# Linear attention, then a mixture of experts: attention outputs as dimensions by tokens in 64-by-32 tiles of TensorE, denominators apart by way of DRAM, and another order of the last stage

## The chip, the cores and the metric

The kernel runs on one core of a Trainium2 chip. The metric is the device time of one execution in microseconds; lower is better. All tensors are float32.

## The reference, cut to what matters

2048 tokens of 512 dimensions go through a pre-normed attention with 32 heads of 16 dimensions, then through a pre-normed mixture of 8 experts. The change touches the two lines that make `num` and `den`, and the last sums of the experts.

```python
phi_q = concat([softmax(pq), softmax(-pq)], -1)      # 32 features a head
kv  = einsum("bhsf,bhsd->bhfd", phi_k, v)            # 32 x 16 a head
z   = einsum("bhsf->bhf", phi_k)
num = einsum("bhqf,bhfd->bhqd", phi_q, kv)
den = einsum("bhqf,bhf->bhq", phi_q, z)[..., None] + 1e-6
h   = x + (num / den) @ wo
...
out = h + sum over experts of cw * (gelu(norm(h) @ w1) @ w2)
```

## The kernel before

The tokens stand in 16 tiles of 128 (index `t`; four tiles make a block `c` of 512). The attention runs as a software pipeline: in step `i`, `steps` calls each stage function of `STAGES` for the tile `i - lag`, in the order of that list, and then `hook(i)`, which doles out loads, weight preparation and the beginning of the experts. A list scheduler puts the instructions of each engine in their final order; each engine then works through its own in that order. DMAs from HBM are issued by SP's queue.

The keys come first: `k_sum` adds up `kv` and `z` in PSUM, with 17-column weights in four column strips of TensorE; `keys_done` turns them and spreads them over a block-diagonal `kv` of 4 heads by 17 columns (16 of `kv`, one of `z`). For the queries, `q_trans` turns the features into `phT`, features by tokens, 8 groups of 4 heads. `q_num` takes each group of `phT` as the weights (128 by 128) and streams 68 columns of `kv`: tokens by (head, 17) come out in PSUM, VectorE adds 1e-6 to each 17th column, takes the reciprocal and multiplies. `q_otrans` turns that result (four 128-by-128 transposes) and splits it in a high and a low part (`split`: a copy on ScalarE, a subtraction on VectorE), `q_out` multiplies it with `wo`, adds `x` and takes the statistics of the norm; `q_norm` and `q_ntrans` make the experts' input from it.

A product of two float32 matrices is three matmuls on those split parts (`mm3`, lines 66 to 68). The expert stage, from step 36 on, is made of them alone: `quad` makes the hidden blocks, `down` the outputs, with a seven-product scheme on 2-by-2 blocks. `finish` ends it: its last product `m4` is accumulated in `pc` by `last(0)` and `last(1)`, `sum_` adds a quarter of the old output on VectorE, `back` turns it and adds `h`, `store` writes it; `put_out` does the same for four other tiles.

PSUM has eight banks in two pools, `ps` and `pacc`, of four each. SBUF buffers come from the pools `s4` and `s2`; an order lists both as `s_` with a number.

## Time and profile before

| | us |
|---|---|
| median of 3 runs (2435.54 to 2436.19) | 2435.96 |
| the profiled execution | 2435.82 |
| its span in the trace | 2434.1 |
| TensorE busy | 2423.8 (100%) |
| VectorE busy | 2158.1 (89%) |
| ScalarE busy | 1759.7 (72%) |
| GpSimd busy | 495.3 (20%) |
| granted TensorE clock | 1.00 of full speed |

The span runs from the first to the last event of the trace; the execution's own time is 1.7 us longer. Busy time counts an engine as occupied while any instruction of it is open; instructions overlap in their pipelines, so a matmul that lasts 0.39 us can begin every 0.23 us.

### The profile page before, as it was taken

How to read it: one execution, taken by the hardware profiler on the slowest of the kernel's cores; microseconds unless marked ns; L12 is line 12 of the kernel's file. 1: busy time of each engine (PE TensorE's matmuls, PEld its weight loads, DVE VectorE, ACT ScalarE, POOL GpSimd, SP SyncE). 2: the span in 40 equal slices, each digit the busy share in tenths (PEclk: the TensorE clock that was granted, in tenths of full speed). 3: DMA queues.
4: the chain of work that ended last, by engine and by line, in shares of the span. 5: the costliest groups of instructions: out<-in, count | busy, mean ns of one | idle time of the engine just before them, and what ended most of it. 6: DMA issues, size and time to landing. Idle time of an engine off the chain costs nothing.

```text
span 2434.1 us, 33612 instructions
## 1 busy us (share of the span) xinstructions
PE 2423.8 (100%) x12032; PEld 2005.3 (82%) x12032; DVE 2158.1 (89%) x3203; ACT 1759.7 (72%) x2885; POOL 495.3 (20%) x555
## 2 busy tenths in 40 slices
PE   9999999999999999999999999999999999999999
PEld 8888788888888888888888888888888888888887
DVE  8778999899898889989886998988989889898998
ACT  5454578777777777777776877777777777777774
POOL 4583111111111111111110331111111111111111
PEclk9999999999999999999999999999999999999999
DMA  3002357777777787777876987887777877777776
GB/s 118 23 10 93 134 186 145 167 147 161 164 140 166 146 170 157 147 157 150 169 156 173 196 185 160 215 195 160 144 165 145 164 160 145 165 146 168 159 149 165
DMA packets 175240, 369.32 MB, mean 152 GB/s; under 512 B 15168, under 2 KB 81728, under 8 KB 175072
## 3 DMA queue, kind: packets, MB, share of 16 engines
q0 software_dynamic: 62304, 204.50, 49.3%
q1 hardware_dynamic: 112624, 162.41, 20.7%
q8 instruction: 94, 1.54, 0.3%
q14 instruction: 74, 0.61, 0.1%
q10 hardware_dynamic: 144, 0.26, 0.0%
HBM read 158.38 MB, written 216.60 MB: 154 GB/s over the span
## 4 chain that ended last, share of the span: by engine, by line
PE 97%; DVE 1%; ACT 0%; issue 0%; POOL 0%; DMA 0%; SPq 0%; DVEq 0%; ACTq 0%; POOLq 0%
PE pacc L67 16%; PE pacc L66 16%; PE pacc L68 16%; PE ps L66 15%; PE ps L67 15%; PE ps L68 15%; PE ps L334 1%; PE pacc L193 1%; PE pacc L305 0%; DVE s L61 0%; PE pacc L271 0%; PE ps L193 0%; PE pacc L757 0%; DMA s<-in_A_wqkv_dram 0%; PE ps L170 0%
## 5 line engine op out<-in xcount | busy, mean ns | idle before, releaser
L61 DVE TENSOR_TENSOR s<-s,s 128x512 fp32r<-128x512 f32 (+1 forms) x800 | 756.0, 958 | 150.5 <-ACT s L60 143.4
L60 ACT ACTIVATE s<-s 128x512 fp32r<-128x512 f32 (+1 forms) x800 | 669.4, 842 | 16.6 <-DVE s L561 7.5
L66 PE MATMUL pacc<-s,s 128*128 128x512 f32 x1732 | 675.6, 391 | 0.0
L68 PE MATMUL pacc<-s,s 128*128 128x512 f32 x1732 | 674.2, 389 | 0.0
L67 PE MATMUL pacc<-s,s 128*128 128x512 f32 x1732 | 674.1, 389 | 0.0
L66 PE MATMUL ps<-s,s 128*128 128x512 f32 x1664 | 651.2, 391 | 0.1
L67 PE MATMUL ps<-s,s 128*128 128x512 f32 x1664 | 647.6, 389 | 0.5 <-DVE s L61 0.5
L68 PE MATMUL ps<-s,s 128*128 128x512 f32 x1664 | 648.0, 389 | 0.0
L595 ACT ACTIVATE s<-pacc 128x512 f32<-128x512 f32 x742 | 439.3, 594 | 192.1 <-PE pacc L68 167.5
L657 ACT ACTIVATE ps<-ps 128x512 f32<-128x512 f32 x448 | 262.4, 586 | 178.2 <-DVE ps L710 104.8
L67 PEld LDWEIGHTS pacc<-s,s 128*128 128x128 f32 x1732 | 325.4, 188 | 67.7 <-DVE s L61 0.8
L68 PEld LDWEIGHTS pacc<-s,s 128*128 128x128 f32 x1732 | 324.9, 188 | 67.5
L66 PEld LDWEIGHTS pacc<-s,s 128*128 128x128 f32 x1732 | 325.1, 188 | 67.3 <-DVE s L61 0.4
L66 PEld LDWEIGHTS ps<-s,s 128*128 128x128 f32 x1664 | 312.4, 188 | 67.3 <-ACT ps L662 1.1
L68 PEld LDWEIGHTS ps<-s,s 128*128 128x128 f32 x1664 | 312.4, 188 | 65.5
L67 PEld LDWEIGHTS ps<-s,s 128*128 128x128 f32 x1664 | 312.3, 188 | 64.6 <-DVE s L61 1.0
L658 DVE TENSOR_TENSOR s<-ps,s 128x512 f32<-128x512 f32 x448 | 303.3, 686 | 47.2 <-ACT ps L657 43.4
L597 POOL DMA_DIRECT2D acc0m<-s x182 | 156.1, 857 | 822.4 <-ACT s L595 796.6
L597 POOL DMA_DIRECT2D acc1m<-s x175 | 150.7, 861 | 784.0 <-ACT s L595 762.4
L561 DVE TENSOR_TENSOR s<-s,s 128x1024 f32<-128x1024 f32 x220 | 268.5, 1220 | 0.1
L662 ACT ACTIVATE ps<-ps 128x512 f32<-128x512 f32 x226 | 132.2, 585 | 74.2 <-PE ps L68 74.2
L535 DVE TENSOR_TENSOR s<-s,s 128x1024 fp32r<-128x1024 f32 x112 | 136.3, 1217 | 0.0
(137 smaller groups left out, 1757.7 us busy)
## 6 DMA issues: line engine op xcount, KB each, us to landing
acc0m<-s POOLq DMA_DIRECT2D x192, 512.0 KB, 5.6
acc1m<-s POOLq DMA_DIRECT2D x182, 512.0 KB, 5.7
s<-in_B_w_dram SPq DMA_DIRECT2D x112, 512.0 KB, 4.3
s<-in_B_w_dram SPq DMA_DIRECT2D x224, 256.0 KB, 5.8
s<-cwT SPq DMA_DIRECT2D x16, 512.0 KB, 5.5
s<-in_A_x_dram SPq DMA_DIRECT2D x31, 256.0 KB, 3.9
h<-s SPq DMA_DIRECT2D x16, 256.0 KB, 2.0
s<-h SPq DMA_DIRECT2D x16, 256.0 KB, 5.7
```

The costliest lines, as they stand in the source:

```text
L60: nc.scalar.activation(hi, src, AF.Copy)
L61: eng.tensor_tensor(lo, src, hi.bitcast(F32), op=ALU.subtract)
L66: nc.tensor.matmul(out_, al, bh, start=first, stop=False, skip_group_check=True)
L67: nc.tensor.matmul(out_, ah, bl, start=False, stop=False, skip_group_check=True)
L68: nc.tensor.matmul(out_, ah, bh, start=False, stop=last, skip_group_check=True)
L535: nc.vector.tensor_tensor(sl, s, sh.bitcast(F32), op=ALU.subtract)
L561: nc.vector.tensor_tensor(B[out_], B[a], B[b], op=ALU.subtract)
L595: nc.scalar.activation(e[:, d], p[d], AF.Copy)
L597: nc.gpsimd.dma_start(macc[h, m], e, accum_op=ALU.add)
L657: nc.scalar.activation(src, src, AF.Gelu_apprx_tanh)
L658: nc.vector.tensor_tensor(B[b][:, q % 2], src, CW[h, e][:, int(b[2]) - 1], op=ALU.mult)
L662: nc.scalar.activation(dst, src, AF.Copy)
```

## The change

`keys_done` now makes two things: `kv`, with rows of 4 heads and 32 columns (the 16 dimensions of two heads side by side, the other pair of heads zeroed by `pmask`), and `z`, shifted copies of which pick the denominators of one tile into its own row. `q_den`, new, runs once for each block of four tiles: 32 matmuls in four column strips add all 32 heads by 4 tiles into one PSUM tile of 128 rows by 128 tokens; VectorE adds 1e-6 and takes the reciprocal, SP writes 64 KB to DRAM (`rden`) and reads it back in four DMAs that repeat each row for the 16 dimensions of its head. `q_num` takes `kv` as the weights and `phT` as the moving side: 16 matmuls of 64 rows by 32 columns of weights and 128 columns of tokens, so that dimensions by tokens come out; VectorE multiplies two halves by the reciprocals. No transposes are needed after it: `q_osplit` splits. `load_wo` loads `wo` with its rows in the order that comes out. The stages have new lags and a new order, and `hook` begins the experts one step earlier. In `finish` the old output is added into `pc` before the last product, `sum_` is a copy on ScalarE, and `back(0)` and `back(1)` go ahead of `last(0)`.

```diff
@@ -257,6 +257,8 @@
+    HP = HG // 2
+    RW = P // 2
     CT = P // (2 * Dh)
@@ -306,7 +308,15 @@
-    kv = consts.tile([P, NG, HN], F32, name="kv")
+    DW = P // KD
+    ZP = HG * TC + TC - 1
+    PD = HP * Dh
+    kv = consts.tile([P, NG, PD], F32, name="kv")
+    pmask = consts.tile([P, HP], F32, name="pmask")
+    rolled = consts.tile([P, HG], F32, name="rolled")
+    for a in range(HG // HP):
+        nc.gpsimd.tensor_copy(rolled[:, a * HP:(a + 1) * HP], hmask[:, (1 - a) * HP:(2 - a) * HP])
+    nc.gpsimd.tensor_tensor(pmask, hmask[:, :HP], hmask[:, HP:], op=ALU.add)
@@ -316,36 +326,87 @@
                 nc.scalar.activation(kvs[r], kvp[r, :NB * P], AF.Copy)
+        z = st["z"] = s2((P, NG, 2 * DW))
+        nc.gpsimd.memset(z, 0.0)
         p = ps()
             nc.tensor.transpose(p[:, b * P:(b + 1) * P], kvs[:, b * P:(b + 1) * P], ident)
-        pv = p[:, :NB * P].rearrange("p (g f) -> p g f", g=NG)[:, :, :DE].rearrange("p g (x d) -> p g x d", x=1)
-        m = hmask.rearrange("p (x a y) -> p x a y", x=1, y=1)
-        nc.vector.tensor_tensor(kv.rearrange("p g (a d) -> p g a d", a=HG), pv.to_broadcast([P, NG, HG, DE]),
-                                m.to_broadcast([P, NG, HG, DE]), op=ALU.mult)
+        pv = p[:, :NB * P].rearrange("p (g f) -> p g f", g=NG)
+        m = pmask.rearrange("p (x b y) -> p x b y", x=1, y=1)
+        nc.vector.tensor_tensor(kv.rearrange("p g (b d) -> p g b d", b=HP),
+                                pv[:, :, :Dh].rearrange("p g (x d) -> p g x d", x=1).to_broadcast([P, NG, HP, Dh]),
+                                m.to_broadcast([P, NG, HP, Dh]), op=ALU.mult)
+        for i in range(2):
+            zi = z.rearrange("p (a i g) c -> p a i g c", i=2, g=2)[:, :, i, :, ZP:ZP + HG * TC:TC]
+            zv = pv[:, :, Dh:DE].rearrange("p (a i g) x -> p a i g x", i=2, g=2)[:, :, i]
+            m = (hmask, rolled)[i].rearrange("p (x y a) -> p x y a", x=1, y=1)
+            nc.vector.tensor_tensor(zi, zv.to_broadcast([P, KH, 2, HG]), m.to_broadcast([P, KH, 2, HG]), op=ALU.mult)
+    rden = [dram.tile([P, P], F32, name=f"rden{c}") for c in range(NT // TC)]
+    def q_den(t):
+        c, j = divmod(t, TC)
+        if j < TC - 1:
+            return
+        p = ps_acc()
+        for j in range(TC):
+            phT = st["ph", c * TC + j]
+            for g in range(2):
+                a = ZP - g * HG * TC - j
+                for k in range(KD):
+                    o = ((k % 2) * KH + k // 2) * DW
+                    nc.tensor.matmul(p[o:o + DW, :P], st["z"][:, 2 * k + g, a:a + DW], phT[:, 2 * k + g, :],
+                                     start=(j == 0 and g == 0), stop=(j == TC - 1 and g == 1),
+                                     tile_position=(0, o), skip_group_check=True)
+        d = s2((P, P))
+        nc.vector.tensor_scalar(d, p[:, :P], 1e-6, None, op0=ALU.add)
+        nc.vector.reciprocal(d, d)
+        st["den", c] = [s4([P, KH, 512]) for _ in range(2)]
+        nc.sync.dma_start(rden[c], d)
+        src = rden[c].rearrange("(i a h j) t -> i h a (j t)", i=2, a=KH, h=2 * HG)
+        for i in range(2):
+            for a in range(KH):
+                nc.sync.dma_start(st["den", c][i][:, a], src[i, :, a].unsqueeze(1).to_broadcast([2 * HG, Dh, 512]))
         phT = st.pop(("ph", t))
-        o = st["o", t] = s2()
-        n = NG // 2
-        for b in range(2):
-            p = ps()
-            for i in range(n):
-                nc.tensor.matmul(p[:, i * HN:(i + 1) * HN], phT[:, b * n + i, :], kv[:, b * n + i, :],
-                                 start=True, stop=True)
-            nv = p[:, :n * HN].rearrange("p (h d) -> p h d", d=DE)
-            den = work.tile([P, H // 2, 1], F32, name="den")
-            nc.vector.tensor_scalar(den, nv[:, :, Dh:], 1e-6, None, op0=ALU.add)
-            nc.vector.reciprocal(den, den)
-            nc.vector.tensor_tensor(o[:, b * (D // 2):(b + 1) * (D // 2)].rearrange("p (h d) -> p h d", d=Dh),
-                                    nv[:, :, :Dh], den.to_broadcast([P, H // 2, Dh]), op=ALU.mult)
-    def q_otrans(t):
+        c, j = divmod(t, TC)
+        new = ps_acc if "m" in late else ps
+        p = [new(), new()]
+        for k in range(KD):
+            for g in range(2):
+                for r in range(2):
+                    o = (2 * g + (r + k) % 2) * PD
+                    nc.tensor.matmul(p[k % 2][o:o + PD, (k // 2) * P:(k // 2 + 1) * P], kv[r * RW:(r + 1) * RW, 2 * k + g, :],
+                                     phT[r * RW:(r + 1) * RW, 2 * k + g, :], start=k < 2, stop=True,
+                                     tile_position=(r * RW, o), skip_group_check=True)
         st["r", t] = s2()
         nc.sync.dma_start(st["r", t], x[t * P:(t + 1) * P, :])
-        p = transposed(st.pop(("o", t)), ps_acc())
-        o = st["O", t] = s4([P, 2, KD, P], F32R)
-        split(o[:, 0], o[:, 1], p)
+        o = st["o", t] = s2()
+        ov = o.rearrange("p (a i t) -> p a i t", a=KH, i=2)
+        for i in range(2):
+            nc.vector.tensor_tensor(ov[:, :, i], p[i][:, :KH * P].rearrange("p (a t) -> p a t", a=KH),
+                                    st["den", c][i][:, :, j * P:(j + 1) * P], op=ALU.mult)
+        if j == TC - 1:
+            del st["den", c]
+    def q_osplit(t):
+        o = st.pop(("o", t))
+        O = st["O", t] = s4([P, 2, KD, P], F32R)
+        split(O[:, 0], O[:, 1], o.rearrange("p (k t) -> p k t", k=KD))
+    def load_wo():
+        r = [s4([P, 2, D]) for _ in range(KD // 2)]
+        for k in range(KD):
+            if k % 2 == 0:
+                nc.sync.dma_start(r[k // 2][:, 0, :], wo[k * P:(k + 1) * P, :])
+                continue
+            for c in range(P // PD):
+                a = k * P + (c + 1 - 2 * (c % 2)) * PD
+                nc.sync.dma_start(r[k // 2][c * PD:(c + 1) * PD, 1, :], wo[a:a + PD, :])
+        return r
@@ -832,6 +893,8 @@
         block(1, 1, pc, r22)
+        for d in range(2):
+            nc.vector.tensor_tensor(pc[d], pc[d], r21[:, d], op=ALU.add)
         hs = [load_h(h * HALF + i, s4) for i in range(TC, HALF)]
@@ -854,10 +917,11 @@
             sl = slice(i * 2 * P, (i + 1) * 2 * P)
-            nc.vector.tensor_tensor(r21[:, d, sl], pc[d][:, sl], r21[:, d, sl], op=ALU.add)
-        def back(d, p, i):
+            nc.scalar.activation(r21[:, d, sl], pc[d][:, sl], AF.Copy)
+        def back(d, i):
+            p = ps_acc()
             src = (r11, r21)[d // 2][:, d % 2]
@@ -869,30 +933,25 @@
+        for d in range(2):
+            for i in range(2):
+                back(d, i)
+        for i in range(2):
+            store(0, 2, i)
         last(0)
             put_out(h * HALF + t, [r12, r22], hs[t - TC])
-        p = ps_acc()
         for i in range(2):
             sum_(0, i)
-        for i in range(2):
-            back(2, p, i)
-        for i in range(2):
-            store(2, 3, i)
         last(1)
         for d in range(2):
-            p = ps_acc()
+            if d:
+                for i in range(2):
+                    sum_(1, i)
             for i in range(2):
-                back(d, p, i)
-        for i in range(2):
-            store(0, 2, i)
-        p = ps_acc()
-        for i in range(2):
-            sum_(1, i)
-        for i in range(2):
-            back(3, p, i)
-        for i in range(2):
-            store(3, 4, i)
+                back(2 + d, i)
+            for i in range(2):
+                store(2 + d, 3 + d, i)
         yield
@@ -954,10 +1013,10 @@
     BEGIN = [(1, k_proj), (-2, x_norm), (-1, x_trans), (-1, x_low), (4, k_sum), (2, k_exp), (-3, x_stats), (3, k_feat)]
-    STAGES = [(-1, x_trans), (-2, x_norm), (25, gate_parts), (-1, x_low), (9, q_proj), (3, k_feat),
-              (2, k_exp), (13, q_exp), (1, k_proj), (22, q_otrans), (20, q_num), (4, k_sum),
-              (12, q_sub), (14, q_feat), (27, lambda t: gate_rows(t, 2)), (15, q_trans), (24, q_norm), (25, gate),
-              (23, q_out), (26, lambda t: gate_rows(t, 1)), (24, q_ntrans), (-3, x_stats)]
+    STAGES = [(15, q_feat), (4, k_sum), (-1, x_trans), (-2, x_norm), (1, k_proj), (17, q_trans),
+              (17, q_den), (9, q_proj), (-1, x_low), (3, k_feat), (14, q_exp), (2, k_exp),
+              (11, q_sub), (25, gate), (21, q_num), (-3, x_stats), (24, gate_parts), (23, q_norm),
+              (27, lambda t: gate_rows(t, 2)), (22, q_out), (23, q_ntrans), (21, q_osplit), (25, lambda t: gate_rows(t, 1))]
     late = {}
@@ -972,32 +1031,32 @@
             late["q"] = load_w(wqkv[:, :D])
-        if i == 2:
+        if i == 3:
             late["f"] = fold(late["q"], wq, bd)
-        if 2 <= i < 2 + 2 * KD:
-            run(late["f"], 3)
+        if 3 <= i < 3 + 2 * KD:
+            run(late["f"], 4)
         if i == 17 - 1:
-            late["o"] = load_w(wo)
+            late["o"] = load_wo()
         if 17 <= i < 17 + KD:
             wos.append(wsplit(late["o"][(i - 17) // 2][:, (i - 17) % 2, :]))
-        if i == 30:
+        if i == 25:
             load1(0)
-        if 31 <= i < 31 + 8:
-            if i == 31:
+        if 30 <= i < 30 + 8:
+            if i == 30:
                 late["p"] = prep1(0)
-            run(late["p"], 6)
-        if i == 33:
+            run(late["p"], 4)
+        if i == 32:
             late["x"] = operands(0)
-        if i >= 33:
+        if i >= 32:
             run(late["x"], 2)
-        if i == 36:
+        if i == 35:
             load_cw(0, 0)
             late["m"] = moe()
-        if i == 45:
+        if i == 42:
             late["s"] = spill(1)
-        if i >= 45:
-            run(late["s"], 4)
-        if i >= 36:
+        if i >= 42:
+            run(late["s"], 7)
+        if i >= 35:
             run(late["m"], 4)
@@ -1025,7 +1084,7 @@
     steps(0, 3, NT, BEGIN, hook)
-    steps(3, 33 + NT, NT, STAGES, hook)
+    steps(3, 29 + NT, NT, STAGES, hook)
     for _ in late["m"]:
```

TensorE's row in one step of the attention's second half, before. `L193` are transposes (of the experts' input and of the attention's output), `L334` is `q_num`, `L305` is `q_trans`, `L66` to `L68` are `q_out` (12 matmuls).

```order
L67 MATMUL pacc<-s_2138,s_2378 128x512
L68 MATMUL pacc<-s_2138,s_2378 128x512
L193 MATMUL pacc<-ident,s_2507 128x128 x4
L193 MATMUL pacc<-ident,s_2381 128x128 x4
L334 MATMUL ps<-kv,s_2186 128x68 x8
L305 MATMUL pacc<-ident,s_2315 128x128 x8
L66 MATMUL pacc<-s_1915,s_2462 128x512
```

The same place with the change, in a step that also has a `q_den` (`L359`, four tiles) and a gate's transposes (`L457`); `L307` is `q_trans`, `L381` is `q_num`.

```order
L68 MATMUL pacc<-s_2158,s_2701 128x512
L193 MATMUL pacc<-ident,s_2752 128x128 x4
L307 MATMUL pacc<-ident,s_2262 128x128 x8
L359 MATMUL pacc<-s_2548,s_2030 32x128 x8
L359 MATMUL pacc<-s_2629,s_2030 32x128 x8
L359 MATMUL pacc<-s_2708,s_2030 32x128 x8
L359 MATMUL pacc<-s_2790,s_2030 32x128 x8
L457 MATMUL pacc<-ident,s_2750 128x128 x4
L381 MATMUL ps<-s_2411,kv 32x128 x16
L66 MATMUL pacc<-s_1907,s_2783 128x512
```

One group of four transposes is gone, and `q_num` went from 8 matmuls to 16; in one step of four, 32 matmuls of `q_den` stand ahead of it.

VectorE before, the denominators of one tile (`L338`, `L339`), the division (`L340`) and the norm (`L188`) that the next transposes of TensorE wait for:

```order
L338 TENSOR_SCALAR den<-ps 128x16
L183 TENSOR_SCALAR rs<-mv 128x1
L338 TENSOR_SCALAR den<-ps 128x16
L339 RECIPROCAL den<-den 128x16 x2
L340 TENSOR_TENSOR s_2547<-ps,den 128x256 x2
L188 TENSOR_SCALAR s_2589<-s_2371,mv,rs 128x512
```

VectorE with the change, from the second `q_den` (`L363`, `L364`) to the first multiplication (`L389`) that needs its reciprocals, read back into `s_2460`; the pair with `s_2129` still uses the block before. `L414` is the addition of `x` in `q_out`.

```order
L363 TENSOR_SCALAR s_2457<-pacc 128x128
L364 RECIPROCAL s_2457<-s_2457 128x128
L389 TENSOR_TENSOR s_2509<-ps,s_2129 128x2x128
L389 TENSOR_TENSOR s_2509<-ps,s_2130 128x2x128
L188 TENSOR_SCALAR s_2512<-s_2283,mv,rs 128x512
L61 TENSOR_TENSOR s_2541<-s_2509,s_2541 128x512
L206 TENSOR_REDUCE mx<-s_2467 128x32
L414 TENSOR_TENSOR s_2368<-pacc,s_2368 128x512
L207 TENSOR_REDUCE mx<-s_2467 128x32
L181 BN_STATS bn<-s_2368 128x6
L389 TENSOR_TENSOR s_2588<-ps,s_2460 128x2x128
```

On SP's queue this is (`L366` the write, `L370` the reads, `L385` the loads of `x`, `L415` the stores of `h`):

```order
L415 DMA h_85<-s_2283 128x512
L366 DMA rden_137<-s_2457 128x128
L385 DMA s_2507<-in_A_x_dram 128x512
L370 DMA s_2460<-rden_137 128x1x512 x2
L370 DMA s_2461<-rden_137 128x1x512 x2
L385 DMA s_2586<-in_A_x_dram 128x512
```

The per-tile reciprocals are gone; each block's reciprocals now pass through DRAM between two places of VectorE's row.

TensorE's last rows before, where `L863` is `back`:

```order
L68 MATMUL ps<-s_23607,s_23604 128x512
L66 MATMUL ps<-s_23607,s_23604 128x512
L67 MATMUL ps<-s_23608,s_23604 128x512
L68 MATMUL ps<-s_23607,s_23604 128x512
L863 MATMUL pacc<-ident,s_23443 128x128 x3
L863 MATMUL pacc<-ident,s_23447 128x128 x2
L863 MATMUL pacc<-ident,s_23443 128x128
L863 MATMUL pacc<-ident,s_23447 128x128 x2
L863 MATMUL pacc<-ident,s_23443 128x128 x4
L863 MATMUL pacc<-ident,s_23447 128x128 x2
```

And with the change, where `L927` is `back`:

```order
L67 MATMUL ps<-s_23747,s_23742 128x512
L68 MATMUL ps<-s_23746,s_23742 128x512
L66 MATMUL ps<-s_23754,s_23751 128x512
L67 MATMUL ps<-s_23755,s_23751 128x512
L68 MATMUL ps<-s_23754,s_23751 128x512
L66 MATMUL ps<-s_23754,s_23751 128x512
L67 MATMUL ps<-s_23755,s_23751 128x512
L68 MATMUL ps<-s_23754,s_23751 128x512
L927 MATMUL pacc<-ident,s_23592 128x128 x8
```

Fourteen transposes followed the last product (a row with x4 merges neighbours), now eight do.

## Rows read from the trace of the kernel before

**Rows 1.** The page's first part: busy time of each engine, its share of the span, and its instructions.

```profile
PE 2423.8 (100%) x12032; PEld 2005.3 (82%) x12032; DVE 2158.1 (89%) x3203; ACT 1759.7 (72%) x2885; POOL 495.3 (20%) x555
```

**Rows 2.** The page's fourth part: the chain of work that ended last, by engine.

```profile
PE 97%; DVE 1%; ACT 0%; issue 0%; POOL 0%; DMA 0%; SPq 0%; DVEq 0%; ACTq 0%; POOLq 0%
```

**Rows 3.** The waits of TensorE over the whole span: who waited for whom; us in total, times, longest.

```profile
PE pacc L305 <- POOL s L215: 1.6, 2, 1.4
```

**Rows 4.** The timeline of TensorE in one step of the attention's second half: start, duration, line, shapes, count (fp32 matmuls of plain float32 stand as two records each, transposes as one).

```profile
195.59 1.04 PE L193 MATMUL pacc<-ident,s 128*128 128x128 f32 x8
196.46 1.90 PE L334 MATMUL ps<-kv,s 128*128 128x68 f32 x16
198.20 1.04 PE L305 MATMUL pacc<-ident,s 128*128 128x128 f32 x8
199.00 0.47 PE L66 MATMUL pacc<-s,s 128*128 128x512 f32 x1
199.31 0.40 PE L67 MATMUL pacc<-s,s 128*128 128x512 f32 x1
...
201.85 1.03 PE L193 MATMUL pacc<-ident,s 128*128 128x128 f32 x8
```

**Rows 5.** Groups of TensorE's instructions by shape: busy us, mean ns of one; the first is of the three split matmuls, the last of the gate's, in four column strips.

```profile
L66 PE MATMUL pacc<-s,s 128*128 128x512 f32 x1732 | 675.6, 391 | 0.0
L334 PE MATMUL ps<-kv,s 128*128 128x68 f32 x256 | 30.8, 271 | 0.0
...
L383 PE MATMUL pacc<-s,wg_pad 128*32 128x512 f32 x32 | 4.3, 605 | 0.0
```

**Rows 6.** The timeline of TensorE around one gate product (`L383`, four matmuls of 32 columns in four column strips, two records each).

```profile
214.81 1.01 PE L334 MATMUL ps<-kv,s 128*128 128x68 f32 x8
215.75 1.07 PE L383 MATMUL pacc<-s,wg_pad 128*32 128x512 f32 x8
216.74 0.66 PE L193 MATMUL pacc<-ident,s 128*128 128x128 f32 x4
```

**Rows 7.** The timeline of TensorE around one `k_sum` (`L271`, 32 matmuls of 17 columns in four column strips, two records each).

```profile
148.70 0.39 PE L68 MATMUL ps<-s,s 128*128 128x512 f32 x1
149.02 0.73 PE L271 MATMUL pacc<-s,s 128*17 128x32 f32 x64
149.68 1.09 PE L305 MATMUL pacc<-ident,s 128*128 128x128 f32 x8
```

**Rows 8.** Groups of VectorE's instructions by shape: busy us, mean ns of one.

```profile
L213 DVE TENSOR_REDUCE s<-s 128x64 f32<-128x1024 f32 x32 | 38.3, 1212 | 9.7 <-ACT s L255 9.7
...
L214 DVE RECIPROCAL s<-s 128x64 f32<-128x64 f32 x32 | 16.7, 536 | 0.0
L340 DVE TENSOR_TENSOR s<-ps,den 128x256 f32<-128x256 f32 x32 | 12.7, 414 | 0.0
...
L339 DVE RECIPROCAL den<-den 128x16 f32<-128x16 f32 x32 | 6.9, 234 | 0.0
...
L338 DVE TENSOR_SCALAR den<-ps 128x16 f32<-128x16 f32 x32 | 5.0, 162 | 6.8 <-PE ps L334 6.7
...
L865 DVE TENSOR_TENSOR s<-pacc,s 128x256 f32<-128x256 f32 x8 | 3.0, 416 | 0.5 <-PE pacc L863 0.5
```

**Rows 9.** Stretches of the span: bounds, length, then the busy time of each engine, the clock, the DMA share and GB/s.

```profile
165.00:215.00 50.00, 50.00 (x335) 44.81 (x333) 42.32 (x103) 23.54 (x39) 31.05 (x25) 1.00 0.13 43
215.00:255.00 40.00, 40.00 (x285) 34.72 (x285) 31.21 (x102) 15.51 (x34) 8.03 (x8) 1.00 0.36 114
255.00:315.00 60.00, 58.50 (x294) 45.15 (x293) 56.52 (x116) 38.87 (x71) 5.12 (x8) 1.00 0.37 128
315.00:355.00 40.00, 40.00 (x180) 33.01 (x179) 39.52 (x59) 32.38 (x53) 4.83 (x8) 1.00 0.61 201
```

**Rows 10.** The waits of VectorE between 165 and 255 us.

```profile
DVE den L338 <- PE ps L334: 6.7, 6, 2.3
DVE s L353 <- PE pacc L68: 6.3, 7, 2.3
```

**Rows 11.** DMA issues between 160 and 260 us: KB each, median us from issue to landing.

```profile
s<-in_A_x_dram SPq DMA_DIRECT2D x12, 256.0 KB, 2.9
h<-s SPq DMA_DIRECT2D x11, 256.0 KB, 2.0
```

**Rows 12.** The timeline of SP's queue: the issue of a store of `h` and of a load of `x`.

```profile
196.60 0.33 SPq L354 DMA_DIRECT2D h<-s  x1
197.03 0.37 SPq L345 DMA_DIRECT2D s<-in_A_x_dram  x1
```

**Rows 13.** The timeline of TensorE at the end of the span: the last matmul of a product, and the last transposes.

```profile
2427.23 0.39 PE L68 MATMUL ps<-s,s 128*128 128x512 f32 x1
2427.46 1.45 PE L863 MATMUL pacc<-ident,s 128*128 128x128 f32 x10
...
2430.46 0.44 PE L863 MATMUL pacc<-ident,s 128*128 128x128 f32 x2 [0.89 <-DVE s L865]
```

**Rows 14.** The timeline of VectorE at the end of the span.

```profile
2418.79 0.69 DVE L799 TENSOR_TENSOR s<-ps,s 128x512 f32<-128x512 f32 x1 [1.95 <-PE ps L68]
...
2427.66 0.42 DVE L857 TENSOR_TENSOR s<-ps,s 128x256 f32<-128x256 f32 x1 [0.15 <-PE ps L68]
...
2430.93 0.42 DVE L865 TENSOR_TENSOR s<-pacc,s 128x256 f32<-128x256 f32 x1 [0.53 <-PE pacc L863]
```

## The prediction, made before the changed kernel ran

> **What bounds the kernel now.** I read the engines first: TensorE is open all the time, VectorE 89% of it [rows 1]. Busy time alone proves little, so the chain that ended last comes next: 97% of it is TensorE [rows 2], and of all TensorE's waits the longest, in two pieces, sums to 1.6 us [rows 3]. The kernel is bound by the number and pitch of TensorE's instructions; whatever leaves its row shortens the span, as long as the other engines keep up. So I price the row first, and then ask of VectorE whether it can follow.
>
> One step of the attention's second half reads like this [rows 4]: eight transposes in 0.87 us (195.59 to 196.46; four turn the attention's output), `q_num` in 1.74 us (to 198.20), `q_trans`, and 12 matmuls of `q_out` at about 0.23 us each. The reader should take differences of starts here, not durations.
>
> **What leaves TensorE.** For each of 16 tiles `q_num`'s 1.74 us and half of 0.87 us: 2.17 us, in all 34.8 us.
>
> **What comes.** No row shows a tile of 64 rows; two shapes bound it. The gate's product has four matmuls of 512 columns in four column strips, two records each: 0.99 us from its start to the next [rows 6]. Its records last 605 ns where one of the split matmuls lasts 391 [rows 5] at a pitch of 0.23, so a float32 pass streams its 512 columns in about 0.44 us, and the four strips run side by side (eight in a row would need 3.5 us). Two rounds of 0.45 us and 0.1 us around them make the 0.99; for 128 columns that is 0.113 us a round. `k_sum` tells the price of going into strips and out: it starts 0.32 us after a matmul that usually takes 0.23, so 0.09 us to enter, and its 16 rounds of 32 columns (0.028 us each, 0.45 us) take 0.66 us [rows 7]. I take 0.17 us for both ways, overhead of small instructions included.
>
> `q_den` has 64 records in four strips: 16 rounds of 0.113 plus 0.17, 1.98 us, four times: 7.9 us.
>
> `q_num` has 32 records for each tile. Its 16 matmuls use eight tiles of the array, and each run of eight in the program touches each once. With all eight side by side it needs four rounds: 0.45 + 0.17 = 0.62 us, 9.9 us in all. With four, as the strips show, 1.07 us, 17.1 us in all. With two, 1.98 us (31.7); with none, 3.79 us (60.6). I take eight: in the gate's product each partition feeds four streams at once without a loss, and eight tiles of 64 rows also ask four streams of each partition. What is new is that two row halves write each PSUM partition at the same time, in different banks.
>
> The Trainium skill, "TensorEngine Tiling (Array Packing)", section "Restrictions and Gotchas", says that different row tiles cannot access the same PSUM bank simultaneously. In this kernel both row halves of one `k` write the bank `p[k % 2]`, at different partitions; no run here shows such a pair. By that rule, read for the whole bank, neighbours in the program take turns, and the sum would be the one with two tiles or with none.
>
> TensorE's sum: -34.8 + 7.9 + 9.9 = -17.0 us (four side by side: -9.8).
>
> **The end.** After the last product's last matmul starts, at 2427.23 [rows 13], VectorE still works until 2431.35 [rows 14], 4.1 us, because additions of the old output, transposes that wait for PSUM (0.89 us) and the accumulation into `h` alternate. With the change eight transposes follow, and two copies on ScalarE. From the same rows: 0.43 us until the product can be read (2427.23 to 2427.66), 0.42 for each of two copies of 256 columns, 0.47 from a transpose's start to its reader's (2430.46 to 2430.93), 0.42 for the reader: 2.2 us. That saves 1.9; six transposes (0.109 us each) now stand ahead of the last product and cost 0.65. Net -1.3 us. The two additions of the old output into `pc` (2 x 0.69) fall into a gap of 1.95 us that VectorE has before 2418.79 [rows 14]; without it they would delay the operands of `m4` by up to 1.4 us.
>
> **VectorE.** Removed are `L338`, `L339`, `L340`: 5.0 + 6.9 + 12.7 = 24.6 us [rows 8]. Added are 32 multiplications of 128x256 (as `L865`, 0.416: 13.3 us), four reciprocals of 128 columns (twice `L214`, 1.07: 4.3), and small ones of about 1.3. Net -5.7 us. Between 165 and 255 us it is busy 73.5 of 90 us [rows 9], and of the 16.5 idle 13.0 are waits for TensorE [rows 10]. After the change 67.8 us of work meet 73 us of TensorE: 5.2 us of room. Behind it there is none: 56.5 of 60 and 39.5 of 40 us are busy [rows 9].
>
> Into that room come the waits for the denominators. After `q_den` ends: about 0.2 us for the addition, 1.07 for the reciprocal, 0.33 to issue the write, 2.0 to land [rows 11, 12], then two reads (0.37 each) and 2.9 to land: the first half is there after 7.2 us, with a load of `x` between write and reads 7.6. In the first block a reduction of 1.21 us [rows 8] stands ahead of the reciprocal: 8.4. Counted from the new order with the prices above, the block's first `q_num` is through TensorE 6.9 us after `q_den` (first block), 8.0 (second), 6.2 (third: gate transposes 0.44, a `q_num` 0.62, `q_out` 2.72, three lots of transposes 0.44 + 0.44 + 0.88, its own 0.62) and 5.3 (fourth). VectorE, which works in order, waits 1.5, 0, 1.4 and 2.3 us for the reads, about 5 us. Behind the waiting `L389` stands `L188`, which TensorE's next transposes need, and 12 matmuls of `q_out` (2.7 us) cover most of that. 3.5 us of other waits (16.5 less 13.0) stay. 5 + 3.5 - 5.2 = 3.3 us do not fit and reach TensorE; I take 4, since some waits for TensorE will stay too. Bounds: 0 (the experts' stage absorbs it; over the span VectorE has 11% to spare [rows 1]) and 16 (13.0 + 3.5 + 5 - 5.2: no wait for TensorE shrinks).
>
> **Costed at nothing.** The new lags and the experts' earlier start move instructions, not their number; TensorE's row stays full, and if a stage comes too early its wait shows as TensorE idle, up to the 1.6 us of [rows 3]. `wo` in ten pieces costs SP 2.6 us more, five steps ahead of the first `q_out`. GpSimd's zeroing of `z` lies in a queue that is busy 31 of 50 us [rows 9].
>
> **Sum.** -17.0 - 1.3 + 4 = -14.3. The profiled execution took 2435.82 us, 0.14 below the median of the runs: 2421.5 us.
>
> **Rivals.**
> - Four tiles side by side. For it: four is what the strips show. TensorE gives 9.8, the end 1.3, and VectorE is pressed less (charge 2 to 4): 2427 to 2429 us. Chance 0.25.
> - VectorE becomes the bound, because the denominators come late or its waits do not shrink: a charge of 8 to 16 eats the gain: 2425.5 to 2433.5, typically 2431. For it: no room from 255 us on [rows 9]. Against it: its idle time before is mostly TensorE's lateness. It decides if a block's reads take over 9 us from `q_den`'s end. Chance 0.18.
> - The row halves take turns at a PSUM bank: two at a time 31.7 us for `q_num`, TensorE +4.8, the end -1.3: 2439 us; none at a time +33.7: 2468. This is the slower side; it decides at 1.7 us for each `q_num` ((34.8 - 7.9) / 16), where the gain is gone. Against it: at any one partition the two halves write different banks. Chance 0.10.
>
> **How the numbers follow.** The forecast (eight tiles, charge 0 to 8) has 0.47 and its own range 2417 to 2426. The range 2416 to 2432 adds the four-tile case and most of the VectorE case, and leaves out the turns at the bank and the worst of VectorE. A change under 0.2% (4.9 us, about what a measurement of this kernel can tell) ends between 2431.1 and 2440.8: 0.11 from the VectorE case and the milder turns. Faster has 0.47 + 0.25 + 0.07 = 0.79, slower 0.10.
>
> **What the profile after would show.** `q_num`'s 32 records within 0.62 us from its start to the next instruction (1.07: four tiles; 2 and more: turns). `q_den` 2.0 us. VectorE waiting for a DMA at `L389` in up to three blocks, 1 to 2 us each; no TensorE wait over 2 us between 165 and 315 us. The last product's end to VectorE's last instruction 2.2 us instead of 4.1. The prediction is wrong if TensorE shows waits that sum to over 10 us before 320 us, or if `q_num` is longer than 1.1 us.

## The result, and the profile after

The changed kernel takes 2449.61 us in the median (2448.71 to 2452.03), the kernel before beside it 2436.07: a ratio of 1.0058, 95% interval 1.0047 to 1.0069. It is slower by 13.5 us where 14.3 less were forecast. The profiled execution took 2452.03 us. Its page still shows TensorE almost always open, and VectorE no less busy than before; in the chain that ended last VectorE now has 3% and DMA 2%, where [rows 2] has 1% and 0.

```profile
PE 2419.0 (99%) x12480; PEld 1991.0 (81%) x12480; DVE 2158.6 (88%) x3147; ACT 1763.4 (72%) x2891; POOL 494.3 (20%) x559
...
PE 93%; DVE 3%; DMA 2%; POOL 1%; issue 1%; ACT 0%; SPq 0%; DVEq 0%; POOLq 0%
```

The stretches answer to [rows 9] (the same columns; the first was not shown of before, where TensorE was busy 33.37 of these 35 us at clock 1.00). From 130 to 315 us TensorE is idle for 24.0 us, before for 3.1, and the granted clock is below 1 in all four; after 315 us all is as before.

```profile
130.00:165.00 35.00, 30.99 (x385) 24.91 (x384) 27.24 (x40) 17.82 (x28) 28.57 (x21) 0.91 0.01 1
165.00:215.00 50.00, 42.14 (x453) 32.45 (x453) 35.13 (x60) 19.91 (x33) 29.57 (x23) 0.94 0.33 104
215.00:255.00 40.00, 35.93 (x414) 27.21 (x413) 29.66 (x70) 17.19 (x37) 9.71 (x9) 0.89 0.36 115
255.00:315.00 60.00, 51.90 (x445) 39.96 (x444) 50.73 (x107) 31.59 (x55) 4.22 (x7) 0.94 0.42 134
```

Who waits: first VectorE between 165 and 255 us (compare [rows 10]), where waits for the read-back have taken the place of most waits for TensorE, and waits for ScalarE's copy of the query projection have come that were not there before; then TensorE between 120 and 340 us (compare [rows 3]), mostly for what stands behind those waits in VectorE's row.

```profile
DVE s L389 <- DMA s<-rden: 12.0, 5, 3.3
DVE mx L206 <- ACT s L285: 6.7, 2, 4.2
```

```profile
PE pacc L66 <- DVE s L61: 6.2, 5, 4.6
PE pacc L193 <- DVE s L188: 4.2, 2, 3.7
PE ps L66 <- DVE s L389: 3.5, 2, 3.1
PE pacc L66 <- DVE s L414: 3.2, 1, 3.2
PE pacc L307 <- ACT s L308: 2.6, 1, 2.6
```

The first block shows it. On TensorE's timeline the `q_den` ends at 167.54; the second `q_num` (at 178.52, of the block's second tile) is followed by a stand of 3.09 us, and the split matmuls behind it start 0.43 us after one another instead of 0.23.

```profile
165.65 1.95 PE L359 MATMUL pacc<-s,s 128*32 128x128 f32 x64
167.54 0.50 PE L66 MATMUL ps<-s,s 128*128 128x512 f32 x1
...
178.52 0.67 PE L381 MATMUL ps<-s,kv 64*32 64x128 f32 x32
182.28 0.61 PE L66 MATMUL ps<-s,s 128*128 128x512 f32 x1 [3.09 <-DVE s L389]
182.69 0.63 PE L67 MATMUL ps<-s,s 128*128 128x512 f32 x1
183.11 0.63 PE L68 MATMUL ps<-s,s 128*128 128x512 f32 x1
```

SP's queue issues the write at 170.37 and the four reads from 172.00 to 174.66. VectorE's timeline has the first half at 177.39 and the second at 181.80, both at the end of a wait for the DMA: 9.9 and 14.3 us after `q_den`'s end. Two loads of `x` (`L385`, 256 KB each) follow the reads on the same queue from 174.75 on.

```profile
170.37 0.35 SPq L366 DMA_DIRECT2D rden<-s  x1
172.00 2.66 SPq L370 DMA_DIRECT2D s<-rden  x4
```

```profile
177.39 0.42 DVE L389 TENSOR_TENSOR s<-ps,s 128x256 f32<-128x256 f32 x1 [0.88 <-DMA s<-rden]
...
181.80 0.42 DVE L389 TENSOR_TENSOR s<-ps,s 128x256 f32<-128x256 f32 x1 [2.80 <-DMA s<-rden]
```

The small tiles are as forecast: `q_den` runs from 257.76 to 259.76, `q_num` from 260.35 to 260.95, 2.00 and 0.60 us.

```profile
257.76 2.08 PE L359 MATMUL pacc<-s,s 128*32 128x128 f32 x64
259.76 0.66 PE L457 MATMUL pacc<-ident,s 128*128 128x128 f32 x4
260.35 0.67 PE L381 MATMUL ps<-s,kv 64*32 64x128 f32 x32
260.95 0.50 PE L66 MATMUL pacc<-s,s 128*128 128x512 f32 x1
```

At the end the last product's last matmul starts at 2444.56 and VectorE ends at 2446.67, 2.1 us later (forecast 2.2; before 4.1, [rows 13, 14]); from there to the span's end it is 3.6 us (before 2.75), so 1.1 us are gained behind that matmul, where 1.9 were forecast. The transposes that now stand ahead of the last product are not in this. Counted from the 25th split matmul from the end, which comes before them, it is 13.8 us to the span's end (from 2436.43) where it was 14.4 (from 2419.73): 0.5 us net, 1.3 forecast. That matmul before, and then with the change:

```profile
2419.73 0.39 PE L68 MATMUL ps<-s,s 128*128 128x512 f32 x1
```

```profile
2436.43 0.39 PE L68 MATMUL ps<-s,s 128*128 128x512 f32 x1
...
2444.56 0.40 PE L68 MATMUL ps<-s,s 128*128 128x512 f32 x1
...
2445.22 1.45 DVE L929 TENSOR_TENSOR s<-pacc,s 128x256 f32<-128x256 f32 x4 [1.56 <-PE pacc L927]
```

### The profile page after: what moved, and what is told of

Its sections match the earlier page's. It is cut to its first block, busy times and chain, and to the rows that moved or that the text cites. A ratio compares the mean times of both kernels' runs of the same rounds, so it can differ in the third digit from the quotient of the medians.

```text
span 2450.3 us, 34506 instructions
## 1 busy us (share of the span) xinstructions
PE 2419.0 (99%) x12480; PEld 1991.0 (81%) x12480; DVE 2158.6 (88%) x3147; ACT 1763.4 (72%) x2891; POOL 494.3 (20%) x559
## 4 chain that ended last, share of the span: by engine, by line
PE 93%; DVE 3%; DMA 2%; POOL 1%; issue 1%; ACT 0%; SPq 0%; DVEq 0%; POOLq 0%
PE pacc L66 15%; PE pacc L67 15%; PE pacc L68 15%; PE ps L66 15%; PE ps L67 15%; PE ps L68 15%; DMA s<-rden 1%; DVE s L213 1%; DVE s L61 1%; POOL s L215 1%; PE ps L193 0%; SPq L370 0%; DVE s L214 0%; PE pacc L273 0%; DMA rden<-s 0%
## 5 line engine op out<-in xcount | busy, mean ns | idle before, releaser
L61 DVE TENSOR_TENSOR s<-s,s 128x1024 fp32r<-128x1024 f32 (+1 forms) x816 | 768.7, 955 | 151.2 <-ACT s L60 144.0
L60 ACT ACTIVATE s<-s 128x512 fp32r<-128x512 f32 (+1 forms) x816 | 679.6, 839 | 40.4 <-DVE s L389 16.8
L66 PE MATMUL pacc<-s,s 128*128 128x512 f32 x1732 | 678.9, 392 | 9.5 <-DVE s L61 6.2
L68 PE MATMUL pacc<-s,s 128*128 128x512 f32 x1732 | 675.7, 390 | 0.0
L66 PE MATMUL ps<-s,s 128*128 128x512 f32 x1664 | 651.2, 392 | 3.6 <-DVE s L389 3.5
L68 PE MATMUL ps<-s,s 128*128 128x512 f32 x1664 | 648.7, 390 | 0.0
L66 PEld LDWEIGHTS pacc<-s,s 128*128 128x128 f32 x1732 | 326.4, 188 | 83.4 <-DVE s L61 8.5
L68 PEld LDWEIGHTS pacc<-s,s 128*128 128x128 f32 x1732 | 326.5, 188 | 68.4
L66 PEld LDWEIGHTS ps<-s,s 128*128 128x128 f32 x1664 | 312.9, 188 | 70.8 <-DVE s L389 3.4
L68 PEld LDWEIGHTS ps<-s,s 128*128 128x128 f32 x1664 | 312.9, 188 | 65.1
```

Of the source, the lines that this page charges most:

```text
L60: nc.scalar.activation(hi, src, AF.Copy)
L61: eng.tensor_tensor(lo, src, hi.bitcast(F32), op=ALU.subtract)
L66: nc.tensor.matmul(out_, al, bh, start=first, stop=False, skip_group_check=True)
L68: nc.tensor.matmul(out_, ah, bh, start=False, stop=last, skip_group_check=True)
```

## Experiments: the read-back

Theory A: the read-back comes late, TensorE stands behind VectorE, and its clock falls. Rival B: the new order, the tiles or VectorE's load cost the time, and the DMA's wait only marks where it ends.

**Nobody waits for it** (the numerators alone are multiplied, by ones; a tile more at the top moves later lines by two).

```diff
-                                    st["den", c][i][:, :, j * P:(j + 1) * P], op=ALU.mult)
+                                    flat, op=ALU.mult)
```

> The kernel after, in which the products with the denominators' inverses (L389) take a resident tile of ones instead of the tile that is read back. The denominators are still worked out, written and read back, and nobody waits for the reads; what is left out is the division, so the output is that of the numerators alone. Theory A (the wait for the read-back is the loss: TensorE stands still for 3 to 5 us in each of the four blocks of tokens, and its clock falls behind each stand): the four stands go with their slow stretches, about 24 us of the 31 that TensorE lost between 150 and 300 us; 2422 to 2430 us, the granted clock of 165 to 300 us back to 0.98 or more, and one stand of 2.6 and 1.4 us left at 156 to 160 us (the end of the keys' sums). Rival B (the new order of the stages, the small tiles on TensorE or VectorE's added work cost the time, and the wait for the DMA only shows where it ends): 2440 us or more, with VectorE's waits moved to TensorE's tiles and TensorE still short of work at 177, 208, 240 and 272 us.

Measured: 2434.84 us, ratio 0.9995 (0.9986 to 1.0005), between the ranges of A and B. So 14.8 us hang on the read-back, a good half of the miss (13.5 + 14.3 = 27.8 us). The two profiled executions lie 17.6 us apart, and 10.1 of these are idle time of TensorE between 130 and 315 us. The clock is back at 1.00 from 165 us on, but 10.4 us of idle TensorE remain in three stretches; between 120 and 340 us it still waits 5.7 us for VectorE's `L61` and 3.4 for `L188`, and 3.6 at the end of the keys' sums.

```profile
165.00:215.00 50.00, 45.77 (x546) 35.80 (x544) 42.45 (x72) 23.99 (x42) 33.39 (x26) 1.00 0.36 115
215.00:255.00 40.00, 38.03 (x524) 29.24 (x505) 33.60 (x85) 17.89 (x39) 7.30 (x9) 1.00 0.43 140
255.00:315.00 60.00, 55.85 (x341) 43.01 (x340) 57.25 (x107) 40.52 (x69) 4.06 (x7) 1.00 0.43 141
```

**Two queues for the reads.**

```diff
-                nc.sync.dma_start(st["den", c][i][:, a], ...
+                (nc.sync, nc.scalar)[i].dma_start(st["den", c][i][:, a], ...
```

> The kernel after, with the two reads of the second half issued on ScalarE's queue instead of SyncE's, so that two queues carry them. Nothing is left out. Reads limited by what the transfer engines move (1 MB of written tile in a block): the second half lands no earlier than some 13 us behind the denominators, the stands on TensorE stay within 1 us, 2446 to 2451 us. Reads limited by one queue that takes them one behind the other (each issue 0.58 to 0.72 us, transfers in turn): both halves land 9 to 10 us behind, the second half's wait of 2.8 to 3.4 us goes, and 2435 to 2442 us.

Measured: 2455.96 us, ratio 1.0081, above both ranges. Now both halves arrive nearly together, at 180.48 and 181.62, 8.2 and 9.3 us after the first issue; on one queue it was 5.4 and 9.8. In the next two blocks the second half came after 9.4 and 9.1 us, on one queue after 8.9 and 9.5. The megabyte takes about the same time whichever queue carries it, 105 to 115 KB in a microsecond, and sharing only makes the first half later. The loads of `x` move at the same time: from 177 to 181.5 us the changed kernel's DMAs moved 198 GB/s in all. How much sooner the reads would land without these loads no run shows. ScalarE's row pays besides: its next work waits 2.57 us behind its own issues.

```profile
172.31 1.81 ACTq L370 DMA_DIRECT2D s<-rden  x2
174.25 0.63 ACT L60 ACTIVATE s<-s 128x512 fp32r<-128x512 f32 x1 [2.57 <-issue]
```

```profile
180.48 0.42 DVE L389 TENSOR_TENSOR s<-ps,s 128x256 f32<-128x256 f32 x1 [2.58 <-DMA s<-rden]
181.62 0.42 DVE L389 TENSOR_TENSOR s<-ps,s 128x256 f32<-128x256 f32 x1 [0.71 <-DMA s<-rden]
```

**One step more for the reads, then two.**

```diff
-              (11, q_sub), (25, gate), (21, q_num), (-3, x_stats), (24, gate_parts), (23, q_norm),
-              (27, lambda t: gate_rows(t, 2)), (22, q_out), (23, q_ntrans), (21, q_osplit), (25, lambda t: gate_rows(t, 1))]
+              (11, q_sub), (26, gate), (22, q_num), (-3, x_stats), (25, gate_parts), (24, q_norm),
+              (28, lambda t: gate_rows(t, 2)), (23, q_out), (24, q_ntrans), (22, q_osplit), (26, lambda t: gate_rows(t, 1))]
```

> The kernel after, with everything from the numerators on (numerators, split, projection, norm, transposes, gate) one step of about 7.6 us later than the denominators. Nothing is left out. Theory A: the reads land about 9.8 us (first half) and 14.2 us (second half) behind the last denominator product, the numerators then ask for them after some 14 us instead of 6.5: no more than 0.5 us of wait in a block; 2423 to 2431 us. Rival B (the order or the load of VectorE): within 3 us of the kernel after, 2446 to 2452 us. Rival C (the reads are held up by other transfers of the queue, whatever the time given them): the wait moves with them, 2435 to 2445 us.

> The kernel after, with everything from the numerators on, and the experts' own preparation with it, two steps later than the denominators. Nothing is left out. Theory A: no wait for the read-back is left in any block; 2421 to 2429 us, and within 2 us of the kernel with one step. Rival B: 2446 to 2452 us. A side effect that either leaves open: tiles of the last steps are held two steps longer, and the experts begin two steps later, which may cost up to 4 us at 300 to 330 us if the experts' preparation was cover for the last tokens.

Measured: 2441.07 us (ratio 1.0021, 1.0012 to 1.0030) and 2441.31 (1.0020). With two steps no wait for the read-back is left. With one, VectorE still pauses for 1.7 us in front of the first block's second half, at 180.31; the profile puts that down to "issue", but it is 10 us after the first read's issue, where the changed kernel had 9.8, so the landing is the likely cause. Yet only 8.5 us of the 14.8 return: with one step a stand of 4.4 us has come up in front of the transposes of the gate's rows, which wait for VectorE; with two it is 2.6 us there and 3.7 in front of a projection.

```profile
PE pacc L477 <- DVE cw L468: 4.4, 1, 4.4
```

The first time falls into rival C's range, but not by its mechanism, since the waits did not move along; A's ranges are missed by 10 and 12 us, and only its forecast that both kernels agree within 2 us held. There is a second cause.

## Experiments: the other 13 microseconds

**The old order.** The new computation under the table and hook of before, denominators at 16, numerators and all behind them a step later.

```diff
...
+              (2, k_exp), (13, q_exp), (1, k_proj), (23, q_osplit), (21, q_num), (4, k_sum),
+              (12, q_sub), (14, q_feat), (28, lambda t: gate_rows(t, 2)), (15, q_trans), (16, q_den), (25, q_norm), (26, gate),
...
```

> The new computation (denominators apart, 64-row tiles, eight small tiles side by side) under the table of stages and the hook of the kernel before, with the denominators one step behind the transposes (16) and the numerators and all behind them one step later than there (21, 23, 24, 25, 26). Nothing is left out. With one step less to fill, the kernel without waits on the read-back came to 2434.8 us, 13 more than forecast: a stand of 2.6 + 1.4 us where the keys' sums end, and VectorE's bursts. Theory A1 (those 13 us come from the new table: the lags are shorter, so the chains through VectorE, ScalarE and GpSimd have less room): 2421 to 2427 us, no stand over 2 us between 150 and 300. Theory A2 (they come from VectorE's load, which the change does not lessen while TensorE's falls by 17 us): 2431 to 2437 us, with TensorE's idle time in front of tiles that VectorE frees, whatever the table.

Measured: 2453.68 us, outside both ranges: a stand of 5.2 us at the end of the keys' sums and 8.5 us of VectorE's waits for the read-back, which are back although the numerators come a step later than in the changed kernel. So the old table brings no gain and has a longer stand at that place; how much of the 13 us the new one costs this run cannot tell, since the waits for the read-back are in it.

**VectorE's work given to others**, on the kernel with the later numerators: the outputs' low parts to GpSimd; or (with the next edit in) the second norm to ScalarE.

```diff
-        split(O[:, 0], O[:, 1], o.rearrange("p (k t) -> p k t", k=KD))
+        split(O[:, 0], O[:, 1], o.rearrange("p (k t) -> p k t", k=KD), nc.gpsimd)
```

```diff
-        nc.vector.tensor_scalar(xn, src, mv[:, t, 0:1], rs[:, t:t + 1], op0=ALU.subtract, op1=ALU.mult)
+        nc.gpsimd.tensor_scalar(nb, mv[:, t, 0:1], rs[:, t:t + 1], -1.0, op0=ALU.mult, op1=ALU.mult)
+        nc.scalar.activation(xn, src, AF.Identity, bias=nb, scale=rs[:, t:t + 1])
```

> The kernel with the numerators one step later (2441.1 us), in which GpSimd instead of VectorE subtracts for the low parts of the outputs (the split ahead of the projection; 16 times 0.63 to 0.95 us on VectorE). Nothing is left out. Theory A2 (VectorE's load bounds the steps): 4 to 10 us less, 2431 to 2437 us. Theory A1 (the table's short lags): within 2 us of 2441, or slower by up to 5 us, since GpSimd takes some 1.2 us for it, has 7 us of work in a step until 215 us, and the projection waits for the low part.

> The kernel with the numerators one step later and the end of the keys' sums behind the query projection (2437.9 us), in which ScalarE instead of VectorE applies the second norm (16 times 0.54 to 1.58 us, 0.66 in the mean, off VectorE; ScalarE is busy for half of 165 to 315 us). Nothing is left out. Theory A2 (VectorE's load in its dense stretches holds TensorE up): 3 to 8 us less, 2430 to 2435 us. Rival (what is left are single chains, the gate's and the norm's, whoever does the work): 2436 to 2440 us.

Measured: 2448.53 and 2448.38 us, 7.5 and 10.5 slower than what they were made from, and outside all four ranges. These pieces are links of a chain, and another engine is a slower link, so the runs do not show what VectorE's load alone costs. GpSimd takes 1.41 us in the mean for a subtraction that took VectorE 0.87 in the changed kernel. In the second kernel ScalarE, which takes its row in order, waits for GpSimd's factor between 165 and 340 us:

```profile
ACT s L190 <- POOL nb L189: 10.6, 7, 3.6
```

**Places.** The end of the keys' sums moved behind the query projection; then also the first gate rows a step later; both this and the norm on ScalarE; and the first move alone where nobody waits for the read-back.

```diff
-        if t == NT - 1:
-            keys_done()
+    def keys_end(t):
+        if t == NT - 1:
+            keys_done()
...
-              (17, q_den), (9, q_proj), (-1, x_low), ...
+              (17, q_den), (9, q_proj), (4, keys_end), (-1, x_low), ...
...
-(26, lambda t: gate_rows(t, 1))
+(27, lambda t: gate_rows(t, 1))
```

> The kernel with the numerators one step later (2441.1 us), in which the end of the keys' sums (their copies, transposes and masked products) stands behind the query projection of its step instead of ahead of the query transposes. Nothing is left out. If the stand of 2.8 + 1.7 us at 153 to 158 us and the slow clock of about 5 us behind it come from that place: 4 to 6 us less, 2435 to 2437 us, and the granted clock of 150 to 165 us at 0.98 or more. If TensorE has nothing to do there, because the chain through GpSimd and ScalarE is late whatever stands first: within 1.5 us of 2441, and the stand in front of another instruction.

> The kernel of 2437.9 us with the transposes of the first gate rows one step later, since they stood for 4.4 us in front of the gate's weights (L479 for L470), which VectorE makes between the experts' sums (four of 1.2 us). Nothing is left out. If that stand is a matter of place: 3 to 5 us less (4.4 and the slow clock behind it), 2433 to 2435 us. If VectorE's backlog holds the next instruction as well: within 1.5 us of 2437.9, the stand in front of a projection or an expert's product.

> Both of these at once: second norm on ScalarE, first gate rows one step later. Nothing is left out. If both work and add: 2425 to 2431 us, which is less than the kernel before. If VectorE's backlog was the one cause: no more than 1.5 us below the better of the two.

> The kernel in which nobody waits for the read-back (2434.8 us; the division left out, lags as in the kernel after) with the end of the keys' sums behind the query projection. If the 3.2 us that this gave with the later numerators are a place's own: 2431 to 2433 us, which leaves 10 us over the forecast to VectorE's bursts and chains. If the stands share one backlog: within 1 us of 2434.8.

Measured: 2437.89, 2436.87, 2444.72 and 2437.77 us. The second and the third fell where one backlog was to put them, the first between its ranges, the last 2 us above both of its own. The first move takes 3.2 us off one kernel and adds 2.9 to another; the second takes 1.0 where the stand that it removed was 4.4, and in its place TensorE's waits for `L61` grew from 1.4 to 6.3 us. Stands move on instead of going. The best of them, 2436.87, stands at 1.0005 of the kernel before (0.9996 to 1.0014): level, no gain.

**Links left out**, where nobody waits for the read-back: first the low parts, then the norm's application too, then with the keys' end moved.

```diff
-        split(O[:, 0], O[:, 1], o.rearrange("p (k t) -> p k t", k=KD))
+        nc.scalar.activation(O[:, 0], o.rearrange("p (k t) -> p k t", k=KD), AF.Copy)
...
-        st["n2", t] = norm_apply(st.pop(("h", t)), t)
+        st["n2", t] = st.pop(("h", t))
```

> The kernel in which nobody waits for the read-back (2434.8 us), and in which the low parts of the outputs are left out besides (the projection takes the high parts twice, with as many products): 16 subtractions of 0.63 to 1.65 us on VectorE and a link of the chain fewer. The division is left out as there. If VectorE's part in the chain from numerators to gate makes the last 13 us: 2424 to 2430 us, the stands in front of the projection gone. If the small tiles or TensorE's own sum were mis-sized: 2433 to 2435 us.

> The same with the second norm's application left out too (the transposes take the sums as they are; the statistics are still made): 16 operations of 0.54 to 1.58 us on VectorE fewer, and the transposes no longer wait for GpSimd's power. If the chain is the rest: 2421 to 2426 us, the forecast's sum, with no more than the stand at the end of the keys' sums left (4 us and the slow clock behind it). If not: within 2 us of the run without low parts.

> The kernel of 2427.0 us (division, low parts of the outputs and second norm left out; nobody waits for the read-back) with the end of the keys' sums behind the query projection. If the stand there is the remainder over the forecast's sum: 2422 to 2425 us. If the chain through GpSimd and ScalarE is late there whatever stands first: within 1 us of 2427.0, with the stand in front of other instructions at 153 to 160 us.

Measured: 2432.76 us (between its ranges), 2426.99 (1 us above the first) and 2428.25 (outside both, 1.3 above the run it was made from). Leaving out two of VectorE's links, and their work with them, gives 7.8 us (2.1 and 5.8), which leaves 5.5 over the forecast. With both gone TensorE is idle only 4.4 us between 165 and 315:

```profile
165.00:215.00 50.00, 48.26 (x562) 37.84 (x561) 35.58 (x68) 24.90 (x43) 35.23 (x29) 1.00 0.39 120
215.00:255.00 40.00, 38.58 (x555) 30.46 (x554) 27.79 (x70) 19.04 (x41) 3.29 (x6) 1.00 0.50 159
255.00:315.00 60.00, 58.75 (x306) 46.04 (x306) 55.13 (x105) 44.94 (x75) 4.07 (x7) 1.00 0.39 131
```

The rest is the stand at the end of the keys' sums: 3.5 us idle between 130 and 165 us, at a clock of 0.90. The move left the idle time as it was, 3.6 us (clock 0.96): TensorE has no work ready. The last run's timeline shows it in front of the transposes and then of `q_den`; a later `q_den` has got a stand of 3.1 us besides.

```profile
159.79 0.44 PE L335 MATMUL ps<-ident,s 128*128 128x128 f32 x2 [2.34 <-DVE s L328]
...
162.34 3.37 PE L363 MATMUL pacc<-s,s 128*32 128x128 f32 x64 [1.23 <-DVE s L345]
```

**A step for each link**, VectorE's work unchanged; then a step for the denominators too.

```diff
...
+              (11, q_sub), (28, gate), (22, q_num), (-3, x_stats), (27, gate_parts), (25, q_norm),
+              (31, lambda t: gate_rows(t, 2)), (24, q_out), (26, q_ntrans), (22, q_osplit), (29, lambda t: gate_rows(t, 1))]
...
```

> The kernel of 2436.9 us (numerators one step later, end of the keys' sums and first gate rows moved) with a step of its own for each link: projection two steps behind the numerators, norm and transposes a step further each, gate and experts two steps later. Nothing is left out, VectorE's work is the same. If the chain's length against a step is what holds TensorE up: 2427 to 2433 us, no stand over 1.5 us between 165 and 300 us. If VectorE's amount of work is: 2435 to 2439 us, with stands of the same sum in front of other tiles.

> The kernel with a step for each link (2440.1 us), with the denominators a step later than the query transposes whose features they take, and numerators and all behind them one step later again. Nothing is left out. If the two stands in front of the denominators (2.5 and 4.9 us, with the slow clock behind each) are what was left: 2427 to 2432 us, faster than the kernel before. If VectorE's delay only comes out in front of another instruction: 2436 to 2441 us.

Measured: 2440.12 and 2437.88 us, the first 1 us above the range of VectorE's amount, the second inside that of a delay that comes out elsewhere. In the first the stands behind low parts and norm are gone, others have come, up to 4.9 us in front of `q_den` for a PSUM tile that VectorE had not yet added up. Neither is free of the read-back: VectorE waits 2.6 us for it in the first kernel and 6.9 in the second.

```profile
DVE s L391 <- DMA s<-rden: 6.9, 3, 3.4
```

The first kernel's timeline of VectorE ahead of the 4.9 us, and GpSimd's at the same time:

```profile
206.29 2.16 DVE L188 TENSOR_SCALAR s<-s,mv,rs 128x512 f32<-128x512 f32 x1 [0.20 <-POOL rs L184]
...
211.11 2.15 DVE L61 TENSOR_TENSOR s<-s,s 128x512 fp32r<-128x512 f32 x1
...
214.38 0.55 DVE L188 TENSOR_SCALAR s<-s,mv,rs 128x512 f32<-128x512 f32 x1 [0.33 <-POOL rs L184]
```

```profile
206.23 1.94 POOL L215 TENSOR_TENSOR s<-s,s 128x1024 f32<-128x1024 f32 x1
210.78 1.93 POOL L215 TENSOR_TENSOR s<-s,s 128x1024 f32<-128x1024 f32 x1 [2.61 <-DVE s L214]
```

The norm takes 0.55 us, or 2.16 when GpSimd's multiplication, begun 0.06 us earlier, runs to 208.17: it ends 0.28 us behind it. The subtraction of 2.15 us ends 0.55 us behind the next one. For the subtraction that is a price of the change: the outputs' low part now has both operands in SBUF, where it had one in PSUM; the norm's operands are as they were. From 165 to 315 us, the subtractions and the norm of before and then of the kernel where nobody waits for the read-back (of its 21 subtractions 5 are not of the outputs, as the 5 of before):

```profile
L61 DVE TENSOR_TENSOR s<-pacc,s 128x512 fp32r<-128x512 f32 x16 | 10.9, 680 | 1.6 <-ACT s L60 1.6
L61 DVE TENSOR_TENSOR s<-s,s 128x512 fp32r<-128x512 f32 x5 | 3.5, 707 | 0.0
L188 DVE TENSOR_SCALAR s<-s,mv,rs 128x512 f32<-128x512 f32 x16 | 9.9, 618 | 2.2 <-POOL rs L184 1.9
```

```profile
L61 DVE TENSOR_TENSOR s<-s,s 128x512 fp32r<-128x512 f32 x21 | 17.8, 846 | 1.3 <-ACT s L60 1.0
L188 DVE TENSOR_SCALAR s<-s,mv,rs 128x512 f32<-128x512 f32 x16 | 12.0, 747 | 1.5 <-POOL rs L184 1.5
```

These 37 took 24.3 us and now take 29.8: 5.5 us more, 3.4 on the subtractions and 2.1 on the norm, nearly as much as the change was to save on VectorE (5.7); over the whole span it is 4.7. All the lengthened ones lie before 220 us, while GpSimd is busy. No run puts the operand back into PSUM, so what this costs in time is not shown apart; leaving the outputs' subtractions out gave 2.1 us. The Trainium skill, "SBUF — State Buffer", section "SBUF: two separate sides", states it as a rule: a VectorE instruction with two SBUF inputs (against a GpSimd one that reads SBUF) or in a two-port mode, and a GpSimd instruction, take a shared pair of ports exclusively, and the one that starts first has it for its whole length. The rows of the subtraction agree; whether the norm's operation is in a two-port mode no row shows. The forecast did not weigh it.

## Why the prediction was wrong

- **TensorE's sum, -17.0: its prices right.** `q_num` 0.60 us for 0.62 and `q_den` 1.89 to 2.00 for 1.98, so eight tiles run side by side. The row halves do not take turns at a bank, though both write the bank `p[k % 2]`: the rule that the prediction drew from the Trainium skill ("TensorEngine Tiling (Array Packing)", section "Restrictions and Gotchas"), read for the whole bank, would have made it 1.98 us or more. The end gave 0.5 net for 1.3.
- **The landing of the reads: the step that failed first.** "Then two reads (0.37 each) and 2.9 to land" priced a transfer that is alone. Four of 256 KB share the transfer engines, with two loads of `x` behind them: issues of 0.58 to 0.72 us, the first half 5.4 us after its first issue, the second 9.8. From `q_den`'s end 9.9 and 14.3 us, where 8.4 was worked out for the first half and nothing for the second. The rival's own threshold of 9 us was passed, but its price, 8 to 16, was too small: in the forecast's terms the charge came to 31.8 (13.5 + 17.0 + 1.3). The runs put 14.8 us on these waits.
- **The clock: left out.** The sum had no term for it. Counted from the timeline between 120 and 340 us, 35 starts from one split matmul to the next take 0.4 us or more instead of 0.23, 7.5 us more in all (before: one, 0.2); they follow stands of 2.6 to 4.6 us. Transposes and small tiles are not in that count. In five pieces, 26.6 us together, the clock is at 0.50 and TensorE busy for 20.4 us (us, busy time, clock, DMA share and GB/s):

```profile
158.70:165.40 6.70, 5.36 (x14) 0.50 0.01 2
182.60:185.90 3.30, 2.88 (x7) 0.50 0.00 0
...
sum 26.60, PE 20.44; mean PE 4.09
```

Half of that, about 10 us, is what the clock cost (an estimate). The profiled execution is 16.2 us longer than before's: 20.9 more idle and 10 for the clock leave about 15 us that the row and the end really saved, where the forecast had 18.3; where the other 3 went stays open but for the end's 0.8.
- **VectorE's room: wrong in size and kind.** The forecast let 5.2 us of room absorb the waits, after 5.7 us less work. VectorE's busy time did not fall (2158.6 us, before 2158.1): the subtractions and norms took 2.5 us more over the span, and the instructions that left (`L338` to `L340`) had been priced by their durations, 24.6 us, where they took 19.4 from one start to the next. Waits of 6.7 us for the query projection stood in the room besides. "12 matmuls of `q_out` (2.7 us) cover most of that" failed: `L61` and `L188` make 10.4 of the 23.8 us that TensorE waits between 120 and 340 us, where the forecast named 10 in all as a sign of being wrong. VectorE was not full meanwhile: with nobody waiting for the read-back it is idle for 7.6 of the 50 us from 165 on. Whether its amount of work or the order of its single links costs the 13 us the runs do not separate: work left out gave 7.8 us, work given to slower engines lost 7.5 and 10.5, and a step more for each link with the same work gave nothing.
- **The new lags, "costed at nothing": not nothing.** At the end of the keys' sums, where the forecast allowed the 1.6 us of [rows 3], TensorE stands for 2.6 + 1.4 us, with a stretch at the slow clock behind it. Since the old table has 5.2 us there, it is not shown whether the lags or the new computation makes this stand.

With both links left out that kernel is 9.5 us above the forecast without its charge of 4. Idle time between 130 and 315 us (7.9 us, before 3.1), the clock of 0.90 over the 35 us to 165 (at most 3.5 us) and the end's missing 0.8 make 9.1 of these, an estimate. What would make TensorE's work ready in time at those places was not settled, nor whether an order exists that brings the gain in; eleven more kernels that compute everything came to 2437 to 2456 us.
